# A first batch that loads keys and queries before values, softmaxes half of its heads without a subtraction pass and mixes heads in pairs, and a last row finished by columns

## The chip, the cores and the metric

The kernel runs on one core of a Trainium2 chip. The metric is the device time of one execution in microseconds (us). Before the change three runs took 468.88, 469.86 and 471.57 us; the median is 469.86 us. TensorE (PE in the profile) multiplies matrices and writes to PSUM; VectorE (DVE) and ScalarE (ACT) work on PSUM and SBUF; GpSimd (POOL) issues the input loads, SyncE (SP) the output stores and the transposing transfers.

## What is computed

Linear attention with projected keys and values, followed by two ReLU mixers, for 8 batches, 8 heads, 1024 rows and a head width of 64:

```python
k_proj = np.einsum('ks,bhsd->bhkd', E, k)      # 1024 rows of keys become 64
v_proj = np.einsum('ks,bhsd->bhkd', F, v)
scores = scale * np.matmul(q, k_proj.transpose(0, 1, 3, 2))
scores = scores - np.max(scores, axis=-1, keepdims=True)
attn = np.exp(scores)
attn = attn / (np.sum(attn, axis=-1, keepdims=True) + 1e-09)
x = heads_joined(np.matmul(attn, v_proj))      # 1024 x 512 per batch
h = np.maximum(x.T @ w_tok1, 0.0) @ w_tok2     # mixes the 1024 rows
u = x + h.T
out = u + np.maximum(u @ w_ch1, 0.0) @ w_ch2   # mixes the 512 columns
```

All inputs are float32 in memory; the loads turn them into bf16, and all products are in bf16 with float32 sums.

## The kernel before, in words

Each batch has two stages. `front(b)` runs from the loads of k, v and q to u and its transpose uT; `channel(b)` is the column mixer and the store. The 1024 rows lie as 128 partitions by NSI = 8, and pairs of these eight share a 128-wide tile (NT = 4).

**Front of the first batch.** Its loads come in chunks of two heads (`CHUNKS0`), in the order k, q, v for each chunk (L272). E and F are loaded by SP (L329), cast (L339), transposed (L347) and copied to `EFT_sb` (L351). `project_first` makes the key projection (L449, copied to `kbd` at L465) and the value projection (L457, copied to `vbd` at L470); each value product is made twice, for the upper and the lower 64 partitions of PSUM, with 64-column weights. `attend(h)` transposes q on PE (L484, copied at L494), makes the scores (L501), takes the row maximum (L510) and subtracts it (L511) on DVE, takes the exponential on ACT (L517), and transposes the result on PE (L536, copied to eT at L539). Heads then come in `GROUPS` of three, three and two: `sums_of` (L558) gives the row sums, which `invert` turns into 1/(sum + 1e-9) (L545, L546); `weigh` (L578) multiplies eT by the projected values, and a multiplication on DVE (L590) writes x. `tok1` (L610) mixes rows for the group's columns, `tok2_of` (L640) mixes them back and adds x by one more product with the identity (L644); its result is copied to u (L653), transposed (L665) and copied to uT (L672).

**Fronts of the other batches** take all eight heads, transpose exponentials and u by transposing transfers on SP's queue (L528, L701), from batch 2 on q too (L726), and add x on DVE (L691).

**Channel.** `up(sj, cc)` (L791) multiplies four rows of tiles by a 128-column slice of w_ch1; the ReLU writes gT (L247 on ACT, L249 on DVE). `down(si)` (L810) sums 12 products with w_ch2 into a full 512-column bank; DVE adds u (L820), SP stores 256 KB (L825).

**What sets the order.** Nothing runs in program order by itself. Each step is an `op` with the engines that may take it, an assumed duration, the ops it needs, and a priority; `Planner.plan` simulates the engines and the load queue with these assumed costs, picks the op that can start earliest (ties by priority), assigns buffers and PSUM banks, and writes out one fixed order for each engine. On the chip an engine follows this order whatever the true durations are. A front has priority level 2b, a channel 2b + 3; inside the first front a `rank` moves whole steps ahead or back (`RK`). All loads hang on one another in the order in which they are made (`load`, `behind`), and go through POOL's one queue: first batch, w_tok1, w_tok2, both halves of w_ch1 (L287), batch 1 in halves of four heads, and then loads held back by a gate (`later`), a one-element copy on POOL (L306) that waits for a late step: w_ch2 (L311) behind the first batch's uT, batch 2 behind the last eT of batch 1, and so on.

Of the kernel before, what the change touches and what calls it, by code (L numbers as in the profile page):

```python
# [10 lines left out]
BF16 = mybir.dt.bfloat16  # L11
# [3 lines left out]


# [43 lines left out]
class Planner:  # L60
# [19 lines left out]
    def plan(self, start):  # L80
# [7 lines left out]
        dma = 4.5  # L88
        ready = [o for o in self.ops if not o.waiting]
        order = []  # L90
        while ready:
# [28 lines left out]
            elif e == "PE":  # L120
                free[e] = t + w
                end = t + w + AFTER[e] + (SLACK if o.prio[0] > 0 else 0.0)
            elif e == "SP":
                free[e] = t + w
                dma = max(t + 1.0, dma) + o.dma
                end = dma + 1.0 + (DMA_SLACK if o.prio[0] % 2 == 0 else 0.0)
            else:
                free[e] = t + w - 0.08
                end = t + w + AFTER[e] - 0.08 + (SLACK if o.prio[0] > 0 else 0.0)
# [16 lines left out]
def kernel(  # L146
# [33 lines left out]
    RK = (-4, 3, 60)  # L180
# [27 lines left out]
    EFT_sb = sb.tile([P, NSI, 2 * KP], BF16, name="EFT_sb")  # L208
# [72 lines left out]
    CHUNKS0 = [(h, h + 2) for h in range(0, H, 2)]  # L281
    for c in CHUNKS0:
        for w in "kqv":
            load_in(0, w, *c, prio=(0, len(pl.ops)))

# [3 lines left out]
    ld_wt1 = load_w(wt1_sb, moe_w_tok1.rearrange("(p si) t -> p si t", p=P), S * DT * 4)  # L289
    ld_wt2 = load_w(wt2_sb, moe_w_tok2.rearrange("(tc p) s -> p tc s", p=P), S * DT * 4)  # L290
    ld_wc1 = []
    for c in range(0, DC, DC // 2):
        cs = slice(c, c + DC // 2)
        ld_wc1.append(load_w(
            wc1_sb[:, :, cs], moe_w_ch1.rearrange("(dc p) c -> p dc c", p=P)[:, :, cs], DM * DC * 2))
    CHUNKS1 = [(0, H // 2), (H // 2, H)]
    for c in CHUNKS1:
        for w in "kvq":
            load_in(1, w, *c, prio=(0, len(pl.ops)))

    ld_wc2 = []

    def later(b, whats, buf, of, dep):

        if b < B:
            gate = op({"POOL": 0.1}, lambda e: nc.gpsimd.tensor_copy(out=mark, in_=of()), [dep], [],  # L306
                      [buf], prio=(2 * b - 2, 0, len(pl.ops)))
            for w in whats:
                if w == "w":
                    ld_wc2.append(load(  # L310
                        lambda: nc.gpsimd.dma_start(  # L311
                            out=wc2_sb, in_=moe_w_ch2.rearrange("(cc p) d -> p cc d", p=P)),
                        (0, len(pl.ops)), DM * DC * 4, [gate]))
                else:
                    load_in(b, w, 0, H, (2 * b - 2, 0, len(pl.ops)), [gate])

# [5 lines left out]
    eft = []  # L322

    def staged(dt):
# [6 lines left out]
            (), [stage] if i == 0 else [], [stage], (-1, i), 0.3)  # L331
        for i, w in enumerate((E, F))
    ]
    for g in range(2):
# [9 lines left out]
        def ef_t(e, g=g, pb=pb):  # L344
# [7 lines left out]
            out=EFT_sb[:, sl, :], in_=b16(pb, 4, P)), [o], [], [pb], prio=(0, -9, g)))  # L352
# [7 lines left out]
    def front(b):  # L360
# [20 lines left out]
        def project(h0, h1):  # L381
# [54 lines left out]
            for h in range(h0, h1):  # L436
                kbd_at[h] = last

        def project_first(h0, h1):
# [14 lines left out]
            def vmm(e):  # L454
                for si in range(NSI):
                    for r in range(2):
                        nc.tensor.matmul(  # L457
                            f32(vb_, n * D)[r * KP : (r + 1) * KP], EFT_sb[:, si, KP : 2 * KP],
                            vin_.t[:, h0:h1, si, :], start=(si == 0), stop=(si == NSI - 1),
                        )  # L460
# [3 lines left out]
            for r in range(2):  # L464
                ok = op(either(n * KP, "f32"), lambda e, r=r: copier(e)(  # L465
                    out=bd.t[0][r * KP : (r + 1) * KP, a, :, r * KP : (r + 1) * KP],
                    in_=f32(kb_, n, KP)[r * KP : (r + 1) * KP]), [ok], [], [kb_, bd], pr())
            ov = op({"PE": 0.1 * NSI}, vmm, eft + [landed[b, "v", h0]], [vb_], [vin_, bd], pr())
            for r in range(2):
                ov = op(either(n * D, "f32"), lambda e, r=r: copier(e)(  # L470
                    out=bd.t[1][r * KP : (r + 1) * KP, h0:h1, r * SU : r * SU + D],
                    in_=f32(vb_, n, D)[r * KP : (r + 1) * KP]), [ov], [], [vb_, bd], pr())
            for h in range(h0, h1):
                kbd_at[h] = ok
                v_at[h] = [ov]

        def attend(h):
# [28 lines left out]
            os_ = op({"PE": 0.056 * NT}, scm, [oq, kbd_at[h]], [sc, mx, sh, ex], [qT, bd], pr())  # L506
# [15 lines left out]
            om = op({"DVE": 2 * dve(512) + 0.06}, smax, [os_], [], [sc, mx, sh], pr())  # L522

            oe = op({"ACT": act(512)}, expo, [om], [], [sh, ex], pr())
# [16 lines left out]

        sums_at, rdG = {}, {}
# [5 lines left out]
        def sums_of(g):  # L548
            heads = GROUPS[g]
# [19 lines left out]
        def weigh(g, t):  # L569
            heads = GROUPS[g]  # L570
            n = len(heads)
            pb = Buf(bankA)
            rd = rdG[g] if first else Buf(rd_pool)
# [6 lines left out]
            new = [pb] + ([] if first else [rd]) + ([xb] if (g, t) == (0, 0) else [])  # L580
# [3 lines left out]
            def norm(e):  # L584
                ou = f32(pb, n, 2 * SU).rearrange("p n (s d) -> p n s d", s=2)
                c = t * 2 * n if first else 0
                r = rd.t[:, c : c + 2 * n].rearrange("p (n s o) -> p n s o", s=2, o=1)
                if not first:
# [6 lines left out]
            x_at[g, t] = op({"DVE": (0 if first else 0.41) + dve(n * 128)}, norm,  # L595
# [7 lines left out]
        def tok1(i, heads):  # L603
# [11 lines left out]
            deps = [x_at[g, t] for g, hs in enumerate(GROUPS) for t in range(NT) if set(hs) & set(heads)]  # L615
# [13 lines left out]
        def tok2_of(heads):  # L629
# [3 lines left out]
            for s0 in range(0, NSI, per):  # L633
                pb = Buf(bankA)

                def mm(e, s0=s0, pb=pb):
                    up_ = f32(pb, per, n)
                    for s_ in range(per):
                        for i in range(TC):
                            nc.tensor.matmul(  # L640
                                up_[:, s_, :], wt2_sb[:, i, s0 + s_ :: NSI],
                                hb.t[:, i, a * D : z * D], start=(i == 0), stop=False,
                            )
                        nc.tensor.matmul(  # L644
# [230 lines left out]
```

## Time and profile before

| What | Value |
|---|---|
| median of three runs | 469.86 us |
| profiled execution: its own time, its span | 470.42 us, 468.6 us |
| PE busy, share of the span | 452.0 us, 96% |
| DVE, ACT, POOL busy | 265.7, 177.8, 35.5 us |
| up products L791, down products L810 | 768 each, 128x512 |
| HBM read, written | 59.24 MB, 16.78 MB |
| granted TensorE clock | 1.000 |

The span runs from the first instruction to the last; the profiled execution's own time is 1.8 us longer. A group line of the profile gives code line, engine, operation, tiles written and read, shape and count, and then the busy time, the mean duration of one in ns, and the idle time of the engine just before them with what ended it. A piece of the timeline gives its start and length in us. The busy time of PE is a union of modelled durations, each about 0.2 us with the pipeline's latency, so that close small gaps between products are covered by it; the number of products in a stretch says more. The mark "POOLq" or "SPq" is an instruction that issues a transfer.

### The profile page before, as it was taken

To read this page: it belongs to the slowest core of one execution; us is meant where nothing else is said; L and a number is where in the kernel's file an instruction comes from. 1 tells how busy PE (TensorE), PEld (TensorE's weight loads), DVE (VectorE), ACT (ScalarE), POOL (GpSimd) and SP (SyncE) were. 2 spreads that over 40 slices of the span, in tenths; PEclk is the share of its full clock that TensorE was granted. 3 is DMA by queue.
4 is the path that set the end of the run, shared out by engine and by line. 5 is a ranking of instruction groups with operands and counts; after the bars stand their busy time and mean duration, and the time that the engine had idled before them with its cause. 6 is when DMAs were issued, how large, how long until landed. Compare 5 with 4: busy or idle time off the path is not lost.

```text
span 468.6 us, 7476 instructions
## 1 busy us (share of the span) xinstructions
PE 452.0 (96%) x2908; PEld 236.3 (50%) x2908; DVE 265.7 (57%) x597; ACT 177.8 (38%) x324; POOL 35.5 (8%) x59
## 2 busy tenths in 40 slices
PE   2799999999999999999999999999999999999996
PEld 2686554444544455545544455545554455544442
DVE  3883884537645578537745499527844297521022
ACT  2866761127310671127510373116720375105600
POOL 7520010010000100010000100010000000000000
PEclk9999999999999999999999999999999999999999
DMA  8999949999899987979399996799488221451022
GB/s 157 207 209 207 191 69 194 230 158 227 99 210 185 179 125 129 202 153 203 50 197 149 188 165 98 168 182 224 87 151 189 90 57 34 65 160 46 1 90 91
DMA packets 122580, 68.14 MB, mean 145 GB/s; under 512 B 86704, under 2 KB 113840, under 8 KB 122544
## 3 DMA queue, kind: packets, MB, share of 16 engines
q0 software_dynamic: 28176, 29.36, 40.1%
q1 hardware_dynamic: 94368, 38.29, 38.4%
q8 instruction: 23, 0.38, 0.3%
q14 instruction: 13, 0.11, 0.1%
HBM read 59.24 MB, written 16.78 MB: 162 GB/s over the span
## 4 chain that ended last, share of the span: by engine, by line
PE 93%; DMA 2%; DVE 2%; POOL 1%; issue 1%; ACT 0%; POOLq 0%; DVEq 0%
PE bank L791 36%; PE bank L810 35%; PE bank L610 6%; PE bank L682 5%; PE bank L578 3%; PE bank L501 3%; PE bank L388 3%; DMA in<-in_v_dram 2%; POOL in L272 1%; DVE x L590 1%; PE bank L640 1%; PE bank L484 0%; PE bank L421 0%; PE bank L665 0%; DVE sh L511 0%
## 5 line engine op out<-in xcount | busy, mean ns | idle before, releaser
L791 PE MATMUL bank<-uT,wc_sb 128*128 128x512 bf16 x768 | 179.1, 379 | 0.0
L810 PE MATMUL bank<-wc_sb,gT 128*128 128x512 bf16 x768 | 173.9, 379 | 0.0
L247 ACT ACTIVATE gT<-bank 128x512 bf16<-128x512 f32 x166 | 98.7, 595 | 87.2 <-PE bank L791 87.2
L810 PEld LDWEIGHTS <-gT 128*128 128x128 bf16 x768 | 73.7, 98 | 84.5 <-issue 1.2
L791 PEld LDWEIGHTS <-wc_sb 128*128 128x128 bf16 x768 | 71.6, 98 | 74.2 <-issue 1.2
L820 DVE TENSOR_TENSOR o<-bank,u 128x512 f32<-128x512 f32 x64 | 43.9, 688 | 110.3 <-PE bank L810 110.3
L510 DVE TENSOR_REDUCE mx<-bank 128x8 f32<-128x512 f32 x64 | 43.6, 681 | 27.5 <-PE bank L501 27.4
L590 DVE TENSOR_TENSOR x<-bank,rd 128x384 bf16<-128x384 f32 (+1 forms) x96 | 48.5, 512 | 3.1
L691 DVE TENSOR_TENSOR u<-bank,x 128x512 bf16<-128x512 f32 x56 | 34.4, 680 | 23.7 <-PE bank L682 23.7
L511 DVE TENSOR_TENSOR sh<-bank,mx 128x512 f32<-128x512 f32 x64 | 44.3, 692 | 5.0 <-ACT ex L517 0.5
L517 ACT ACTIVATE ex<-sh 128x512 bf16<-128x512 f32 x64 | 40.1, 627 | 5.8 <-DVE sh L511 3.7
L402 ACT CAST kp<-bank 64x512 bf16<-64x512 f32 (+1 forms) x8 | 4.2, 525 | 90.9 <-PE bank L392 90.9
L247 ACT ACTIVATE hT<-bank 128x512 bf16<-128x512 f32 (+2 forms) x19 | 9.9, 523 | 64.9 <-PE bank L610 64.8
L610 PE MATMUL bank<-x,wt_sb 128*128 128x512 bf16 (+2 forms) x160 | 29.6, 336 | 0.0
L682 PE MATMUL bank<-hT,wt_sb 128*128 128x512 bf16 x112 | 25.3, 379 | 0.0
L249 DVE TENSOR_SCALAR gT<-bank 128x512 bf16<-128x512 f32 x26 | 17.8, 687 | 11.9 <-PE bank L791 11.4
L578 PEld LDWEIGHTS <-eT 128*128 128x128 bf16 x256 | 18.6, 97 | 11.2 <-DMA eT<-ex 0.2
L578 PE MATMUL bank<-vbd,eT 128*128 128x130 bf16 x256 | 23.1, 220 | 0.0
L501 PEld LDWEIGHTS <-qT 128*128 128x128 bf16 x256 | 17.8, 98 | 10.2 <-ACT qT L494 0.6
L501 PE MATMUL bank<-kbd,qT 128*128 128x128 bf16 x256 | 21.8, 219 | 0.5 <-ACT qT L494 0.5
L610 PEld LDWEIGHTS <-wt_sb 128*128 128x128 bf16 x160 | 14.6, 98 | 13.4
L682 PEld LDWEIGHTS <-wt_sb 128*128 128x128 bf16 x112 | 16.1, 144 | 8.4
(63 smaller groups left out, 214.1 us busy)
## 6 DMA issues: line engine op xcount, KB each, us to landing
out_dram<-o SPq DMA_DIRECT2D x64, 256.0 KB, 2.7
in<-in_k_dram POOLq DMA_DIRECT2D x6, 1024.0 KB, 11.0
in<-in_v_dram POOLq DMA_DIRECT2D x6, 1024.0 KB, 15.5
in<-in_q_dram POOLq DMA_DIRECT2D x6, 1024.0 KB, 9.7
wc_sb<-in_moe_w_ch_dram POOLq DMA_DIRECT2D x2, 768.0 KB, 17.2
wc_sb<-in_moe_w_ch_dram POOLq DMA_DIRECT2D x1, 1536.0 KB, 26.4
in<-in_k_dram POOLq DMA_DIRECT2D x4, 256.0 KB, 8.4
in<-in_q_dram POOLq DMA_DIRECT2D x4, 256.0 KB, 8.9
```

What stands on the lines that cost most here:

```text
L247: nc.scalar.activation(out=out, in_=in_, func=ACT.Relu)
L501: nc.tensor.matmul(f32(sc, NT, 2 * KP)[:, t, :], qT.t[:, h, t, :], bd.t[0][:, h // 2, h % 2, :], start=True, stop=True,)
L510: nc.vector.reduce_max(out=mx.t, in_=s_, axis=AX.X)
L511: nc.vector.tensor_tensor(out=sh.t, in0=s_, in1=mx.t[:, :, None].to_broadcast([P, NSI, KP]), op=ALU.subtract,)
L517: nc.scalar.activation(out=ex.t, in_=sh.t.rearrange("p (t s) k -> p t (s k)", s=2), func=ACT.Exp, scale=scale,)
L578: nc.tensor.matmul(ou[:, i], eTs[h].t[:, t, :], bd.t[1][:, h, :], start=True, stop=True)
L590: nc.vector.tensor_tensor(out=xb.t[:, t, heads[0] : heads[0] + n], in0=ou[:, :, :, 0:D], in1=r.to_broadcast([P, n, 2, D]), op=ALU.mult,)
L610: nc.tensor.matmul(f32(pb, n), wt1_sb[:, si, i * P : (i + 1) * P], xrow(si, a, z), start=(si == 0), stop=(si == NSI - 1),)
L682: nc.tensor.matmul(f32(pb, DM), wt2_sb[:, i, si::NSI], hb.t[:, i, :], start=(i == 0), stop=(i == TC - 1),)
L791: nc.tensor.matmul(f32(pb, 4, P), wc1_sb[:, dc, cc * P : (cc + 1) * P], uT.t[:, sj * 4 : (sj + 1) * 4, dc, :], start=(dc == 0), stop=(dc = ...
L810: nc.tensor.matmul(f32(pb, DM), g.t[:, cc, (si % 4) * P : (si % 4 + 1) * P], wc2_sb[:, cc, :], start=(cc == 0), stop=(cc == CC - 1),)
L820: nc.vector.tensor_tensor(out=ob.t, in0=f32(pb, DM), in1=u.t[:, si, :], op=ALU.add)
```

## The change

Parts, in the order of the code:

1. **Load order** (`LOADS`). First batch: q1, k0, q0, k1, k3, k2, v1, q3, v0, q2, then w_tok1, v2, v3, w_tok2, the first half of w_ch1, then batch 1 (k, v, q of the first four heads; v, k, q of the others), and only then the second half of w_ch1.
2. **Later loads** (`GATES`). w_ch2 comes in two halves, one behind the first batch's uT, one behind head 0's eT of batch 1; batch 2 comes behind head 4's eT of batch 1 instead of head 7's. The others keep their places.
3. **Value projection** of the first batch: one product with 128-column weights for two with 64 columns. `EFT_sb` holds F twice for it (two added copies).
4. **Exponentials** of heads 3, 4, 6 and 7 of the first batch (`DIRECT`): DVE takes the maximum and multiplies the 128x8 result by -scale; ACT then takes eight exponentials of 128x64 straight from PSUM with that result as bias. The subtraction is gone.
5. **Pairs** (`GROUPS0`): four groups of two heads for three of three, three and two; row sums for each (`SUMMED`).
6. **Adding x** in groups 0 and 3 (`ADDED`): by DVE on the way from PSUM to u, in two pieces of 256 a bank, for the identity product and a copy.
7. **The last row** of the last batch (`down_by_columns`): 256, 128 and 128 columns, each with its own 12 products, addition and store.
8. The ranks, some assumed costs of the planner, and the dependences of the two halves of `kbd` and `vbd` (both halves now follow the product, before one followed the other). `front(b + 1)` is described to the planner before `channel(b)`.

```diff
+LOADS = ("q1", "k0", "q0", "k1", "k3", "k2", "v1", "q3", "v0", "q2", "wt1", "v2", "v3", "wt2",
+         "wc1a", "K0", "V0", "Q0", "V1", "K1", "Q1", "wc1b")
+GROUPS0 = ((0, 1), (2, 3), (4, 5), (6, 7))
+DIRECT = (3, 4, 6, 7)
+ADDED = (0, 3)
+SUMMED = (0, 1, 2, 3)
+RK = (-30, -3, 63)
+GATES = {(0, "u"): ("w0",), (1, 0): ("w1",), (1, 4): ("v2", "k2", "q2"), (1, "u"): ("k3", "v3"),
...
-    RK = (-4, 3, 60)
...
             def vmm(e):
                 for si in range(NSI):
-                    for r in range(2):
-                        nc.tensor.matmul(
-                            f32(vb_, n * D)[r * KP : (r + 1) * KP], EFT_sb[:, si, KP : 2 * KP],
-                            vin_.t[:, h0:h1, si, :], start=(si == 0), stop=(si == NSI - 1),
-                        )
+                    nc.tensor.matmul(
+                        f32(vb_, n * D), EFT_sb[:, si, KP : 3 * KP],
+                        vin_.t[:, h0:h1, si, :], start=(si == 0), stop=(si == NSI - 1),
+                    )
...
+            def rmax(e):
+                nc.vector.reduce_max(out=mx.t, in_=f32(sc, NSI, KP), axis=AX.X)
+                nc.vector.tensor_scalar(
+                    out=mx.t, in0=mx.t, scalar1=-scale, scalar2=None, op0=ALU.mult)
+
+            def expo_direct(e):
+                s_ = f32(sc, NSI, KP)
+                for si in range(NSI):
+                    nc.scalar.activation(
+                        out=ex.t[:, si // 2, (si % 2) * KP : (si % 2 + 1) * KP], in_=s_[:, si, :],
+                        func=ACT.Exp, bias=mx.t[:, si : si + 1], scale=scale,
+                    )
...
+            if first and h in DIRECT:
+                om = op({"DVE": dve(512) + 0.2}, rmax, [os_], [], [sc, mx], pr())
+                oe = op({"ACT": NSI * 0.15 + 0.08}, expo_direct, [om], [], [sc, mx, sh, ex], pr())
...
+                def add(e, s0=s0, pb=pb):
+                    for s_ in range(0, per, 2):
+                        w = min(2, per - s_)
+                        nc.vector.tensor_tensor(
...
+        def down_by_columns(si, widths):
...
+            for w in widths:
...
+                    for cc in range(CC):
+                        nc.tensor.matmul(
+                            f32(pb, cs.stop - cs.start), g.t[:, cc, (si % 4) * P : (si % 4 + 1) * P],
+                            wc2_sb[:, cc, cs], start=(cc == 0), stop=(cc == CC - 1),
+                        )
...
+                op({"SP": 0.1}, lambda e, cs=cs: nc.sync.dma_start(
+                    out=out.rearrange("b (p si) d -> b p si d", p=P)[b, :, si, cs], in_=ob.t[:, cs]),
...
+            if (b, si) == (B - 1, NSI - 1):
+                down_by_columns(si, (DM // 2, DM // 4, DM // 4))
```

## The prediction

> **What bounds the kernel now.** I read the busy shares and the slices first. Columns of the first lines: busy us, share, instructions; below, tenths of busy time in 40 slices of 11.7 us.
>
> ```profile
> PE 452.0 (96%) x2908; PEld 236.3 (50%) x2908; DVE 265.7 (57%) x597; ACT 177.8 (38%) x324; POOL 35.5 (8%) x59
> PE   2799999999999999999999999999999999999996
> DVE  3883884537645578537745499527844297521022
> ACT  2866761127310671127510373116720375105600
> ```
>
> PE is full from the fourth slice to the last but one; the first three and the last are what is open. The busy time by stretches then says where (columns: stretch, length, busy us and count for PE, weight loads, DVE, ACT, POOL, clock, DMA share, GB/s):
>
> ```profile
> 5.00:10.00 5.00, 1.53 (x13) 1.27 (x14) 1.32 (x3) 2.39 (x2) 4.04 (x6) 1.00 1.15 173
> 10.00:15.00 5.00, 4.55 (x116) 4.03 (x115) 2.22 (x5) 3.38 (x10) 2.65 (x4) 1.00 1.24 205
> 15.00:20.00 5.00, 3.40 (x89) 2.76 (x84) 4.58 (x9) 4.39 (x10) 2.25 (x4) 1.00 1.24 205
> 20.00:25.00 5.00, 4.45 (x107) 3.94 (x104) 4.72 (x12) 4.18 (x10) 2.26 (x4) 1.00 1.12 213
> 25.00:30.00 5.00, 4.71 (x67) 4.40 (x68) 4.83 (x11) 3.36 (x9) 1.48 (x2) 1.00 1.15 210
> 30.00:35.00 5.00, 4.80 (x72) 4.59 (x69) 3.37 (x10) 3.06 (x8) 1.19 (x2) 1.00 1.18 207
> 35.00:40.00 5.00, 4.65 (x71) 4.36 (x70) 1.50 (x4) 3.87 (x8) 0.00 (x0) 1.00 1.25 210
> 60.00:440.00 380.00, 379.32 (x2124) 188.93 (x2123) 221.44 (x506) 135.16 (x236) 17.69 (x29) 1.00 0.78 143
> ```
>
> From 60 to 440 us PE idles 0.7 us in all; nothing there can be shortened but by taking products away. From 15 to 30 us DVE is 94% busy (14.1 of 15 us), ACT 80%, and the loads run at a steady 205 GB/s. So the first front is bound first by arriving loads, then by DVE. The timeline shows where it ends: the last transposes of u, and the first product of the channel stage at 39.92 us.
>
> ```profile
> 39.69 0.40 PE L665 MATMUL bank<-ident,u 128*128 128x128 bf16 x4 [0.35 <-ACT u L653]
> 39.92 0.38 PE L791 MATMUL bank<-uT,wc_sb 128*128 128x512 bf16 x1
> ```
>
> From then on PE always has something, so every us by which the first front ends earlier is a us of the total, as long as the work behind it has its data. At the end, the chain of waits and the timeline show the other open piece:
>
> ```profile
> 443.88 20.73 PE bank L810 x96
> 464.63 0.69 DVE o L820
> ```
>
> The last addition ends at 465.32, its store lands about 2.0 us after its issue (transfers by stretches), and the span ends at 468.6.
>
> **The loads, part 1.** Issue time plus time to landing, asked load by load, gives for the first batch 7.3 (k0), 8.9, 10.2, 11.5, 12.7, 14.0, 15.3, 16.65, 19.05, 20.3, 21.5 and 22.9 us (v3), then w_tok1 25.5, w_tok2 27.85, the halves of w_ch1 31.55 and 35.3, batch 1's six pieces 37.8, 40.4, 42.9, 45.4, 48.0 and 50.5, w_ch2 59.5. POOL issues as many transfers of the same sizes in the same queue, so I put the new order on these slots: the last query chunk (q2) lands at 20.3 instead of q3 at 21.5, w_tok1 at 22.9, v2 and v3 at 24.2 and 25.5 (2.6 us later than v3 before), w_tok2 again at 27.85, w_ch1's first half at 31.55, batch 1 from 34.1 to 46.9 (each 3.7 us earlier), w_ch1's second half at 50.5 instead of 35.3. Scores of heads 2, 3 can start 1.2 us earlier; heads 0, 1, whose q0 moves from 8.9 to 10.2, lose little, since their keys wait for EFT (copied until 10.15) and their scores started at 12.88.
>
> **PE work, parts 3, 5, 6.** The value projection saves nothing: 16 paired half-width products took 0.64 us, 8 full-width ones (L484, the x8 piece) 0.61. The identity products of two groups go: 3 products per row of tiles took 0.247 us at 192 columns, so tok2 cost 16 x 0.082 + 8 x 0.056 = 1.77 us there and costs 16 x 0.056 = 0.90 in a pair: with the columns regrouped, 16 products of 128 are saved, 0.9 us. Tok1 handles the same columns in 64 products instead of 48. None of this binds before 32 us; it is a part of the earlier end below, not added to it.
>
> **DVE and ACT until the last x.** The stretch 10 to 33.8 us holds 19.71 us of DVE and 17.65 of ACT. DVE changes: four subtractions at 0.69 go, four 128x8 multiplications come (nearest row: 128x24, 0.17; I take 0.15), -2.2; 16 multiplications of 0.42 for 8 of 0.55 and 4 of 0.42, +0.6; a fourth inversion, +0.3; two copies of F (nearest row 0.29 for 64x256 bf16), +0.5; additions of group 0, 2 banks x 2 x 0.42, +1.7. Sum 20.6. ACT: eight exponentials of 128x64 are not in the trace. From above: the 64x128 cast, 0.258 each without overlap, 2.06 a head. From below: the ACT rows at 128 and 512 columns (0.277, 0.595) make 0.17 + 0.00083 a column, 0.22 at 64, and two copies in a row (1.07 for two of 0.585) overlap by 0.10, so 0.12 each, 0.96 a head. I take 0.18, in the middle, 1.45 a head: 4 x (1.45 - 0.63) = +3.3; the four copies of group 0's u at 0.477 go to DVE, -1.9. Sum 19.0. So DVE stays the longer one, 0.9 us longer than before, but it starts fuller: in 10 to 15 us it idled 2.8 us for want of scores, and with four heads' q and k there by 12.7 instead of 14 to 16 I expect half of that; with the other 1.3 us of idle time kept, 10 + 20.6 + 1.4 + 1.3 = 33.3, less 0.5 for copies that ACT (19.0 of 23) can take: last x at 32.8 instead of 33.8.
>
> The Trainium skill (ScalarE: Activation LUTs, What ACT_TABLE_LOAD costs) says that an activation whose bias is a per-partition operand takes about 280 ns + 0.833 ns a column, and that neighbours overlap by about 93 ns. That is an estimate of 0.24 us each and 1.9 a head; the 512-column rows here (0.595 to 0.63) lie near the 0.61 that it gives without such an operand and below the 0.71 with one, so no row here shows the surcharge. By the rule ACT would hold 20.8 us, and the third rival below would be near.
>
> **From the last x to the channel stage.** Before, 33.8 to 39.9, 6.1 us, because PE was still busy with the second group's tok1 and tok2 (32.0 to 35.9). With pairs, that work is done two heads at a time and earlier; w_tok2's landing at 27.85 plus 64 + 16 products at 0.056 (4.5 us) ends at 32.4, before the last x is through. What remains is serial: tok1 16 x 0.056 + 0.17 = 1.1, ReLU 0.28, tok2 0.9, addition or copy 0.58 to 0.84, transposes 0.4, copy 0.5: 3.9 us. The channel stage starts at **36.7** instead of 39.9: -3.2. Bounds: 35.2 (exponentials at the low end, last x 1.5 earlier) and 39.3 (at the high end, 4 x 0.6 = 2.4 us more on ACT).
>
> **What the moved half of w_ch1 costs.** Until 50.5 us PE has 12 ups of 4 x 0.216, 10.4 us, and of batch 1 two projections of 0.9, queries and scores of 0.9 for each half: some 14 us for 13.8. I take 0.2 us of idling. If nothing of batch 1 came in time, PE would have done 10.4 us by 50.5, where it did 10.6 before: the move can eat the gain, not turn it into a loss. The split of w_ch2 lands at or after 54.5 and about 59.5, as before; 10.4 us of ups cover 50.5 to 59.5. Batch 2's loads (part 2), released at 67.75 before, come some 8 us earlier.
>
> **The last row, part 7.** PE needs 24 products of 128 more than half as many of 256 do: 12 x (0.109 + 0.056 + 0.056) = 2.65 for 2.59 us, +0.06. The last addition falls from 0.69 to 0.29 (0.42 at 256 columns, 0.69 at 512, carried on), -0.4. The last store moves 64 KB instead of 256: packets of the last 256 KB ran some 0.8 us, so between nothing and 0.6 is saved; I take 0.4. Together -0.75.
>
> The Trainium skill (DMA: Bandwidth & Descriptors, two cost components) gives 2.0 us fixed plus bytes at 436 GB/s; by it the store saves an estimate of 0.45. The trace's 2.0 us for a whole 256 KB store is below its 2.6, so the fixed part is smaller here.
>
> **Sum.** -3.2 + 0.2 - 0.75 = -3.75 us on the profiled execution's 470.42 (span 468.6 and 1.8 around it): 466.67. That execution lay 0.56 above the median of the runs, 469.86, so the forecast is **466.1 us**, own range 464.0 to 467.5.
>
> **Rivals.**
> 1. *The front ends little earlier.* DVE has more to do, not less (20.6 for 19.7), and v3 comes 2.6 us later; if the order holds DVE no fuller than before, the last x stays at 33.8 or slips to 34.5, and only the shorter tail of PE work remains, an end near 38.8. For it: 94% of DVE. Against it: its idle 2.8 us at 10 to 15. 470.42 - 1.1 - 0.75 - 0.56 = 468.0 us. Chance 0.24.
> 2. *The forecast*, 0.62, with ends down to 35.2 (464.4) in it.
> 3. *ScalarE becomes the bound.* Each direct head waits for 2.06 us of ACT where the plan assumed 1.28; ACT cannot hand exponentials on, and qT and eT copies are queued behind them, as PE's transposes of later heads are behind the ones that wait. 4 x 0.78 = 3.1 us late on ACT, and the same again when PE's and DVE's fixed orders wait for the late eT: the channel starts at 36.7 + 6.2 = 42.9, 470.42 + 3.0 - 0.75 - 0.56 = 472.1 us. It turns to a loss when the front ends after 40.65, at 1.94 a head, 0.24 an exponential. For it: ACT already at 80%. Against it: 4 us of ACT are idle before 33.8. Chance 0.14. The skill's rule named above gives this break-even price almost exactly.
>
> **Numbers.** A measurement of this kernel can tell about 0.5% (2.35 us) from no change: faster is below 467.5, slower above 472.2. Rival 1 straddles the first bound, rival 3 the second with its worse half: faster 0.62, same 0.25, slower 0.13. Range 463.8 to 470.8: it takes in the forecast and rival 1 and leaves out most of rival 3.
>
> **What would show it.** The first L791 product near 36.7 us; DVE above 90% from 12 us; an exponential of 64 columns at 0.15 to 0.2 us apart; last x near 33; w_ch1's second half landing near 50 with PE idle under 1 us from 37 to 60; a last addition of 0.3 us and a span that ends 3.2 us after the last product instead of 4.0. Wrong would be a channel start at or after 39, or PE gaps beyond 60 us.

## The result, and the profile after

The changed kernel takes **476.31 us** in the median of six runs (474.33 to 478.84), where 466.1 was forecast: 1.0137 times the time before, with a 95% interval of 1.0101 to 1.0173. It is slower by 6.5 us, and the range given (463.8 to 470.8) doesn't hold it. The profiled execution took 476.23 us, its span 474.4: 5.8 us more than before. A run more than 1.5% longer than the shortest of its kernel is left out of the medians and ratios below: one of e2 (476.32 us), four of e4 (481.07 to 482.50) and one of the kernel before (535.93).

The top of the page of after, its busy line and the slices of PE and ACT:

```profile
PE 452.3 (95%) x2895; PEld 238.3 (50%) x2924; DVE 267.6 (56%) x618; ACT 179.6 (38%) x345; POOL 36.3 (8%) x61
PE   2899998996999999999999999999999999999996
ACT  2886841044510373116621184114730185105600
```

PE's row, all nines from the fourth slice to the last but one before, now has an 8 in the seventh slice and a 6 in the tenth (71 to 83 and 107 to 119 us). That is far behind the first front, in a part of the kernel that the prediction took to be full. What PE waited for after 50 us (line waited at, releaser, total, times, longest):

```profile
PE bank L524 <- DMA qT<-in: 4.2, 1, 4.2
PE bank L619 <- DMA eT<-ex: 1.1, 1, 1.1
```

Before, only a wait of 0.7 us stood in that stretch. The chain of waits of after shows both at their places (start, length, what):

```profile
63.80 8.97 DMA eT<-ex
...
94.74 18.76 DMA qT<-in
...
113.55 0.61 PE bank L524 x4
```

The second is the larger one. A transposing transfer of batch 2's q, half of it (four heads), took 18.8 us to land; the first half took 4.6, and before the change the two took 5.6 and 7.8. What is queued around it is seen in the timeline of SP and POOL (start, us, engine, line, operation):

```profile
91.18 1.76 SPq L783 DMA_TRANSPOSE qT<-in  x1
93.03 1.62 SPq L907 DMA_DIRECT2D out_dram<-o  x2
94.74 9.60 SPq L783 DMA_TRANSPOSE qT<-in  x1
```

```profile
93.19 0.18 POOL L327 COPY mark<-uT 1x1 bf16<-1x1 bf16 x1 [27.08 <-DMA uT<-u]
93.64 0.88 POOL L286 DMA_DIRECT2D in<-in_k_dram  x1 [0.28 <-issue]
```

Batch 3's k and v are held back until batch 1's uT is complete. That now comes at 93.19, between the two halves of q. So two loads of 1 MB each (as written) are issued 1.1 and 0.2 us ahead of the second half (k at 93.64, v at 94.51), and even the instruction that issues the half stays blocked for 9.6 us. Before the change, SP and POOL had it the other way round (the second line is the second half, which is also part of the first):

```profile
93.41 5.43 SPq L726 DMA_TRANSPOSE qT<-in  x2
96.98 1.87 SPq L726 DMA_TRANSPOSE qT<-in  x1
97.27 0.18 POOL L306 COPY mark<-uT 1x1 bf16<-1x1 bf16 x1 [26.39 <-DMA uT<-u]
97.81 0.88 POOL L272 DMA_DIRECT2D in<-in_k_dram  x1 [0.36 <-issue]
```

Both halves were issued first, but the second only 0.8 us ahead of k's load. PE pays twice. Stretches of after (columns as in the table of before, the clock third from the end):

```profile
112.00:114.00 2.00, 0.45 (x5) 0.45 (x6) 0.00 (x0) 0.00 (x0) 0.00 (x0) 0.83 0.86 241
114.00:116.00 2.00, 2.00 (x10) 0.90 (x8) 1.38 (x2) 0.10 (x1) 0.00 (x0) 0.50 0.98 202
116.00:118.00 2.00, 2.00 (x11) 0.95 (x10) 1.38 (x2) 1.54 (x4) 0.00 (x0) 0.82 0.00 0
118.00:120.00 2.00, 2.00 (x14) 1.03 (x13) 1.33 (x2) 2.00 (x5) 0.00 (x0) 1.00 0.41 84
```

After the gap the granted clock is 0.50, and 1.00 again from 118 on; from 114 to 118 that costs 2 x 0.50 + 2 x 0.18 = 1.4 us, and 1.6 with the 0.45 us from the end of the gap to 114. So 4.2 + 1.6 + 1.1 = 6.9 us are lost here, more than the 5.8 by which the span grew. By this count the rest of the change gained 1.1 us in this execution.

The front itself, by the stretches of after:

```profile
10.00:15.00 5.00, 4.68 (x102) 4.25 (x101) 2.87 (x7) 2.23 (x6) 2.57 (x5) 1.00 1.24 205
15.00:30.00 15.00, 12.58 (x236) 10.60 (x230) 12.92 (x37) 14.79 (x54) 5.76 (x8) 1.00 1.17 209
```

From 15 to 30 us ACT, the fourth pair, is busy 14.8 of 15 us, where DVE led before with 14.1; DVE is down to 12.9. The timeline of after has the last x, and the first product of the channel stage:

```profile
32.96 1.41 DVE L631 TENSOR_TENSOR x<-bank,rd 128x256 bf16<-128x256 f32 x4
40.70 1.03 PE L848 MATMUL bank<-uT,wc_sb 128*128 128x512 bf16 x4
```

The last x ends at 34.4 (before 33.8), and the channel starts at 40.7 (before 39.9).

### The profile page after: what moved, and what is told of

It reads as the page before. It is cut to its first block, busy times and chain, and to the rows that moved or that the text cites. A ratio compares the mean times of both kernels' runs of the same rounds, so it can differ in the third digit from the quotient of the medians.

```text
span 474.4 us, 7540 instructions
## 1 busy us (share of the span) xinstructions
PE 452.3 (95%) x2895; PEld 238.3 (50%) x2924; DVE 267.6 (56%) x618; ACT 179.6 (38%) x345; POOL 36.3 (8%) x61
## 4 chain that ended last, share of the span: by engine, by line
PE 87%; DMA 7%; ACT 3%; issue 1%; DVE 1%; SPq 0%; ACTq 0%
PE bank L848 33%; PE bank L891 32%; PE bank L651 5%; PE bank L739 5%; DMA qT<-in 4%; PE bank L524 3%; PE bank L619 3%; PE bank L412 2%; DMA eT<-ex 2%; DMA gT<-in_F_dram 1%; ACT ex L553 1%; PE bank L681 1%; PE bank L507 1%; ACT ex L540 1%; PE bank L722 0%
## 5 line engine op out<-in xcount | busy, mean ns | idle before, releaser
L848 PE MATMUL bank<-uT,wc_sb 128*128 128x512 bf16 x768 | 181.6, 381 | 0.1
L891 PE MATMUL bank<-wc_sb,gT 128*128 128x512 bf16 x729 | 168.4, 379 | 1.4 <-issue 0.2
L261 ACT ACTIVATE gT<-bank 128x512 bf16<-128x512 f32 x170 | 101.0, 595 | 129.8 <-PE bank L848 128.8
L891 PEld LDWEIGHTS <-gT 128*128 128x128 bf16 x756 | 72.8, 98 | 85.9 <-issue 2.5
L533 DVE TENSOR_REDUCE mx<-bank 128x8 f32<-128x512 f32 x60 | 41.0, 684 | 20.2 <-PE bank L524 20.1
L534 DVE TENSOR_TENSOR sh<-bank,mx 128x512 f32<-128x512 f32 x60 | 41.5, 692 | 4.9
L540 ACT ACTIVATE ex<-sh 128x512 bf16<-128x512 f32 x60 | 37.6, 627 | 4.7 <-DVE sh L534 3.5
L651 PE MATMUL bank<-x,wt_sb 128*128 128x512 bf16 (+1 forms) x176 | 29.9, 321 | 0.0
L524 PE MATMUL bank<-kbd,qT 128*128 128x128 bf16 x256 | 22.9, 224 | 4.7 <-DMA qT<-in 4.2
L261 ACT ACTIVATE hT<-bank 128x512 bf16<-128x512 f32 (+1 forms) x18 | 9.7, 536 | 41.0 <-PE bank L651 41.0
L651 PEld LDWEIGHTS <-wt_sb 128*128 128x128 bf16 x176 | 14.8, 98 | 13.2
L263 DVE TENSOR_SCALAR gT<-bank 128x512 bf16<-128x512 f32 x22 | 15.1, 688 | 8.8 <-PE bank L848 8.3
## 6 DMA issues: line engine op xcount, KB each, us to landing
in<-in_v_dram POOLq DMA_DIRECT2D x4, 256.0 KB, 10.6
```

The source lines that it names most:

```text
L261: nc.scalar.activation(out=out, in_=in_, func=ACT.Relu)
L524: nc.tensor.matmul(f32(sc, NT, 2 * KP)[:, t, :], qT.t[:, h, t, :], bd.t[0][:, h // 2, h % 2, :], start=True, stop=True,)
L533: nc.vector.reduce_max(out=mx.t, in_=s_, axis=AX.X)
L534: nc.vector.tensor_tensor(out=sh.t, in0=s_, in1=mx.t[:, :, None].to_broadcast([P, NSI, KP]), op=ALU.subtract,)
L540: nc.scalar.activation(out=ex.t, in_=sh.t.rearrange("p (t s) k -> p t (s k)", s=2), func=ACT.Exp, scale=scale,)
L651: nc.tensor.matmul(f32(pb, n), wt1_sb[:, si, i * P : (i + 1) * P], xrow(si, a, z), start=(si == 0), stop=(si == NSI - 1),)
```

## The experiments

The theory, after reading the two traces: the earlier release of batch 3's k and v puts them ahead of q's transposing transfer, and this collision is the loss. The rivals were that the first front itself comes out later (the direct exponentials, the load order), and that the two stores which now stand between the halves of q delay the second one. Each ratio below is to the kernel before, run on the same chip beside it, whose median was 469.97 to 470.53 us.

**e1: the loads of batch 3 wait for q's transposes.** One gate moved, nothing else.

```diff
-GATES = {(0, "u"): ("w0",), (1, 0): ("w1",), (1, 4): ("v2", "k2", "q2"), (1, "u"): ("k3", "v3"),
+GATES = {(0, "u"): ("w0",), (1, 0): ("w1",), (1, 4): ("v2", "k2", "q2"), (2, "q"): ("k3", "v3"),
...
+            later((b, "q"), qTb, lambda: qTb.t[0:1, 4, 0, 0:1], o)
```

> The changed kernel with one edit: the loads of keys and values of batch 3 wait for the second half of batch 2's q transposes, no longer for batch 1's uT. Theory 'collision' (the 18.8 us landing of that half, issued just after those loads, starves PE by 4.2 us and half the clock for some 4 us costs 1.7 more): that half lands in 5 to 7 us, no PE wait over 1 us at 108 to 114 us, granted clock 1.000, 470.4 us. Rival 'spread' (the earlier loads of batch 2, the late eT and a slower first front cost a little everywhere): 474 us or more, stall or no stall. Rival 'front' (the new first batch loses what is lost): 476 us.

Measured: 468.44 us, ratio 0.9975 [0.9954, 0.9995]; the span of the profiled execution 466.6 us, at a clock of 1.000. The timeline of e1, SP and then POOL:

```profile
90.89 3.03 SPq L783 DMA_TRANSPOSE qT<-in  x1
94.02 1.01 SPq L908 DMA_DIRECT2D out_dram<-o  x2
95.12 3.46 SPq L783 DMA_TRANSPOSE qT<-in  x1
```

```profile
101.19 0.88 POOL L286 DMA_DIRECT2D in<-in_k_dram  x1 [0.28 <-issue]
```

The same two stores stand between the halves, which land 5.0 and 5.5 us after issue, and no wait of PE beyond 50 us is left in the list. So the stores alone are not the cause, and with the collision the loss is gone: 7.8 us of span between the two executions. Not all of the 7.8 is the gate's. The wait of 1.1 us for eT is missing too, and the channel starts at 40.1 instead of 40.7, both at places ahead of the release that was moved.

**e2: both halves of q in one step,** so that no store and no load comes between them; the gates as in the change.

```diff
-            for h0 in range(0, H, 4):
-                o = op({"SP": 3.5}, lambda e, h0=h0: nc.sync.dma_start_transpose(
...
+            def both(e):
+                for h0 in range(0, H, 4):
+                    nc.sync.dma_start_transpose(
...
+            o = op({"SP": 7.0}, both, [landed[b, "q", 0]], [qTb], [qin, qTb], pr(), dma=8 * S * D * 2 / TURN)
```

> The changed kernel with one edit: both halves of a batch's q transposes are one step of the plan, so that no store stands between them on SP. Theory 'collision': the second half is issued before the loads of batch 3 take the queues, lands in 5 to 8 us, 470.4 us. If the loads hit it all the same, although it is issued first: landing over 12 us and 474 to 476 us. Rival 'front': 476 us.

Measured: 469.70 us, ratio 0.9997 [0.9981, 1.0013]; span 467.6. SP issues the two from 91.48 on, 5.38 us for both, the second at 94.64, and POOL k's load at 95.53; the halves land in 5.3 and 9.0 us. The stall of PE is gone with q ahead of the loads, whichever way this is reached. The stores matter only as far as they put the second half behind the loads. e2 is 1.3 us above e1, with intervals that overlap; of the 1.0 us between the two spans 0.9 lie ahead of anything the edit touches (the channel starts at 41.0, in e1 at 40.1).

**e3: the new gates alone,** in a kernel that otherwise has the load order, groups, exponentials, ranks and last row of before (it keeps the full-width value projection and the planner's new costs).

```diff
-GROUPS0 = ((0, 1), (2, 3), (4, 5), (6, 7))
-DIRECT = (3, 4, 6, 7)
-ADDED = (0, 3)
+LOADS = ("k0", "q0", "v0", "k1", "q1", "v1", "k2", "q2", "v2", "k3", "q3", "v3", "wt1", "wt2",
+         "wc1a", "wc1b", "K0", "V0", "Q0", "K1", "V1", "Q1")
+GROUPS0 = ((0, 1, 2), (3, 4, 5), (6, 7))
+DIRECT = ()
+ADDED = ()
...
-RK = (-30, -3, 63)
+RK = (-4, 3, 60)
...
-            if (b, si) == (B - 1, NSI - 1):
+            if False:
```

> Only the changed gates of the later loads (and the full-width value projection); the first batch's load order, groups, exponentials, addition of x and the last row are those of before. Theory 'collision': the plan has the same two stores between the halves of q, so the stall is there too if the timing of batch 1 is alike: 474 to 477 us, second half landing over 12 us. Rival 'front': no loss without the new first front, 470 us.

Measured: 485.58 us, ratio 1.0339 [1.0304, 1.0374]. PE waits 7.5 us for qT, whose second half was issued at 100.73, 1.0 us behind batch 3's k, and landed 19.3 us later; and 4.0 us for eT. Without the new first batch the gates cost over twice as much as with it. So the first batch isn't what made the kernel slower.

**e4: the first batch alone,** with the old places of w_ch2 and batch 2.

```diff
-GATES = {(0, "u"): ("w0",), (1, 0): ("w1",), (1, 4): ("v2", "k2", "q2"), (1, "u"): ("k3", "v3"),
+GATES = {(0, "u"): ("w0", "w1"), (1, 7): ("k2", "v2", "q2"), (1, "u"): ("k3", "v3"),
```

> The changed kernel with the gates of before for w_ch2 and batch 2 (both halves of w_ch2 behind the first batch's uT, batch 2 as k, v, q behind head 7's eT); first batch and last row as changed. Theory 'collision': q of batch 2 lands some 4 us later than in the changed kernel, its halves are issued before the loads of batch 3 or land late with one store between; without the stall 470 to 471 us, what is left is what first batch and last row are worth, within 1 us of nothing. Rival 'front': 475 to 477 us.

Measured: 471.19 us, ratio 1.0032 [1.0015, 1.0050]; the profiled execution, with a span of 471.3, is the longest of the six. In it PE waits 1.5 us for qT (halves landing in 5.4 and 11.5 us) and 0.9 for v. The second half was issued at 101.35 and batch 3's k at 101.41: a dead heat.

**e7: the kernel before, with batch 3's k and v released earlier.** The test from the other side: nothing of the change, only this release.

```diff
-        later(b + 2, "w" if first else "kv", uTb, lambda: uTb.t[0:1, NSI - 1, 0, 0:1], uT_at[b][NSI - 1][-1])
+        sg = 1 if b == 1 else NSI - 1
+        later(b + 2, "w" if first else "kv", uTb, lambda: uTb.t[0:1, sg, 0, 0:1], uT_at[b][sg][-1])
```

> The kernel before with one edit: the loads of batch 3's keys and values wait for the first two of eight tiles of batch 1's uT instead of the last, so they are issued some 5 us earlier, ahead of the q transposes of batch 2. Theory 'collision': one or both q halves land in over 12 us instead of 5.6 to 6.7, PE waits 2 to 7 us for them near 103 to 112 us and then runs at half clock for a few us: 473 to 479 us. Rival (the stall belongs to the changed plan, not to loads ahead of a transposing transfer): 470 us, halves under 8 us.

Measured: 480.4 us, ratio 1.0216 [1.0195, 1.0238]. The timeline of e7:

```profile
91.83 0.88 POOL L272 DMA_DIRECT2D in<-in_k_dram  x1 [0.36 <-issue]
```

```profile
94.29 16.81 SPq L726 DMA_TRANSPOSE qT<-in  x2
```

its chain of waits, with the first half alone:

```profile
94.29 17.25 DMA qT<-in
```

and PE's waits and its stretches:

```profile
PE bank L501 <- DMA qT<-in: 8.8, 1, 8.8
```

```profile
108.00:112.00 4.00, 0.41 (x5) 0.41 (x6) 0.00 (x0) 0.00 (x0) 0.00 (x0) 0.50 1.25 226
112.00:116.00 4.00, 4.00 (x18) 2.05 (x17) 3.45 (x6) 1.11 (x2) 0.00 (x0) 0.51 0.89 308
```

Here no store stands between the halves of q. The first is issued 2.5 us behind k and lands in 17.3 us; its instruction stays blocked for 12.6 us, so the second is issued only at 107.0, and lands in 6.2. 8.8 us of waiting and 4 x 0.49 = 2.0 us at half clock make 10.8, and the span grew by 10.6 (479.2 for 468.6). Loads ahead of the transposes are enough by themselves.

**e5 and e8: no direct exponentials.** e5 is e1 with `DIRECT = ()`; e8 is e5 with the last row as in e6 below.

> The kernel of e1 (batch 3's keys and values behind q's second half) with one more edit: no head of the first batch takes its exponentials straight from PSUM (the subtraction is back for heads 3, 4, 6, 7). Theory 'ScalarE bound' (eight exponentials take 1.75 us where one took 0.63, ACT is 98% busy from 15 to 30 us): ACT falls by 4.5 us there, DVE rises by 2.1, the last x comes up to 1 us earlier, 467.4 to 468.4 us against e1's 468.4. Rival 'DVE bound': DVE is again 94% busy and the first front ends 1 us later, 469 to 470 us. A change of the plan's order elsewhere (q's transposes go ahead of uT's) may cost or give some tenths.

> e1 with both edits of e5 and e6. If both theories hold and add up: 466.8 to 467.8 us, 0.5% under the kernel before. Rival 'DVE bound': 468.5 to 469.5 us.

Measured: 473.88 us, 1.0072 [1.0051, 1.0092], and 472.79 us, 1.0057 [1.0038, 1.0076]. The plan came out in another order, with q's transposes ahead of uT's, and PE waits for k, eT and uT (2.2, 1.8 and 1.5 us in e5). They don't price the exponentials; a kernel with its order kept was needed.

**e9: subtraction, in the order and with the buffers of e6.** Every engine keeps its sequence; only what the two steps do is put back, for heads 3, 4, 6 and 7.

```diff
-                om = op({"DVE": dve(512) + 0.2}, rmax, [os_], [], [sc, mx], pr())
-                oe = op({"ACT": NSI * 0.15 + 0.08}, expo_direct, [om], [], [sc, mx, sh, ex], pr())
+                om = op({"DVE": dve(512) + 0.2}, smax, [os_], [], [sc, mx], pr())
+                oe = op({"ACT": NSI * 0.15 + 0.08}, expo, [om], [], [sc, mx, sh, ex], pr())
```

> The kernel of e6 with every engine's order and all buffers kept, but heads 3, 4, 6 and 7 of the first batch do the subtraction on DVE (0.69 us) and one exponential on ACT (0.63) where e6 has the 128x8 multiplication (0.17) and eight exponentials (1.75). This takes the plan's reshuffling of e5 out. Theory 'ScalarE bound': ACT falls from 98% to about 80% between 15 and 30 us, the first front's last transposes of u come up to 1 us earlier, 467.4 to 468.4 us against e6's 468.4. Rival 'DVE bound': DVE above 93% there, the front ends 0.5 to 1.5 us later, 469 to 470 us.

Measured: a median of 473.48 us over 12 runs, 1.0035 [0.9996, 1.0074], in two groups: 468.34 to 470.68 (3 runs) and 472.17 to 475.29 (9). The profiled execution is of the first, span 466.5, against 466.3 of e6. From 15 to 30 us, e6 and then e9:

```profile
15.00:30.00 15.00, 12.57 (x218) 10.59 (x217) 13.11 (x38) 14.78 (x55) 5.79 (x8) 1.00 1.17 209
```

```profile
15.00:30.00 15.00, 11.49 (x211) 10.13 (x209) 14.39 (x36) 10.50 (x26) 5.90 (x8) 1.00 1.17 209
```

The direct form takes 1.3 us from DVE (third pair) and puts 4.3 on ACT (fourth). The last x ends at 33.9 with it and 34.1 without, and the spans differ by as much, 0.2 us: that is all that the subtraction's removal gives to the front in these two executions. The longer group is another matter (e13).

**e13: e9's kernel once more,** for the trace of one of its longer runs.

> The kernel of e9 once more, for a profile of the slower kind of its executions. Theory 'second collision': a PE wait of 2 to 5 us for eT<-ex at 70 to 78 us, landing of head 7's eT 8 us or more, the granted clock under 1.0 in the stretch behind it, no other wait over 1.5 us after 40 us. Rival: the wait is elsewhere. If the execution is of the faster kind (468 to 470.7 us), the look tells nothing new.

Measured: 474.58 us, span 472.7. Its waits and two of its stretches:

```profile
PE bank L619 <- DMA eT<-ex: 2.8, 1, 2.8
```

```profile
76.00:78.00 2.00, 2.00 (x11) 1.12 (x10) 1.43 (x6) 0.00 (x0) 0.00 (x0) 0.50 1.23 205
78.00:80.00 2.00, 2.00 (x8) 0.73 (x6) 0.85 (x2) 0.00 (x0) 0.00 (x0) 0.67 1.24 205
```

This is the smaller wait of the change's own trace, larger: batch 2's loads, released behind head 4 of batch 1 (POOL issues them from 64.31 on), slow the last eT transposes of the same batch. Head 7's eT lands in 10.7 us; before the change the last one took 2.4.

The first batch has a part in it, which the rival of the next experiment also names. From 15 to 30 us e13 has

```profile
15.00:30.00 15.00, 12.50 (x224) 11.39 (x218) 13.65 (x32) 10.35 (x25) 5.95 (x8) 0.89 1.17 209
```

with a granted clock of 0.89 where e9's shorter execution and e6 had 1.00, and its channel starts at 42.0 instead of 40.5. These 1.5 us, the wait of 2.8 and 2 x 0.50 + 2 x 0.33 = 1.7 at the lower clock make 6.0 of the 6.2 us between the two spans. The later front also brings the collision about: head 7's eT is issued at 65.12 instead of 63.56, while the mark behind head 4 moves only from 63.54 to 63.80. So the loads, 0.5 us behind this eT in e9, are 0.8 us ahead of it here. How much of the 1.5 us is the clock's isn't shown (PE also waited 0.6 us longer for E and F at the start), and the other eight long runs have no trace.

**e12: e9 with batch 2 released behind head 7,** as before the change.

```diff
-GATES = {(0, "u"): ("w0",), (1, 0): ("w1",), (1, 4): ("v2", "k2", "q2"), (2, "q"): ("k3", "v3"),
+GATES = {(0, "u"): ("w0",), (1, 0): ("w1",), (1, 7): ("v2", "k2", "q2"), (2, "q"): ("k3", "v3"),
```

> The kernel of e9 with one more edit: batch 2's loads wait for head 7's eT of batch 1 instead of head 4's. e9's executions fell into two kinds, 468.3 to 470.7 us at a clock of 1.000 and 472 to 475 at 0.992 to 0.995. Theory 'second collision' (batch 2's loads, issued before the last eT transposes of batch 1, stretch them to 9 us or more, as in the changed kernel and in e11, and whether PE then waits long enough to lose its clock hangs on a few tenths): with the later release all executions lie within 2 us of each other, clock 0.998 or more, 468.5 to 471 us, with PE waiting up to 1.5 us for batch 2's values. Rival (the two kinds come from the first batch): two kinds again.

Measured: 470.69 us, 0.9998 [0.9978, 1.0018]; 11 runs from 468.76 to 471.90, batch 2 released at 68.27 in the trace, no wait for eT, and no run above 472. With the release behind head 7 the times of e9 above 472 are gone, so these had the second collision in them. But the expectation (all within 2 us, clock 0.998 or more) wasn't met, and the rival is right in part: four runs took 468.76 to 469.71 us at a clock of 0.999, and six 470.34 to 471.90 at 0.996 (the eleventh 471.08 at 1.000). The profiled one is of the longer kind:

```profile
15.00:30.00 15.00, 12.21 (x215) 11.07 (x214) 13.33 (x32) 10.26 (x24) 5.69 (x8) 0.89 1.17 209
```

Its clock falls in the first front as in e13, and its channel starts at 42.7, 2.2 us later than in e9's; the span is 2.9 longer. In e6 and e10, which have the direct exponentials, all 23 runs had a clock of 0.999 or 1.000. So the direct exponentials give 0.2 us where the clock stays up, but in e9 and e12, without them, it often didn't: the medians of e9 and e6 are 473.48 and 468.44 us.

**e11: the load order of before,** all else as in e6.

> The kernel of e6 with the first batch's loads, weights and batch 1 in the order of before. If the new load order is what shortens the first front: its last transposes of u come 1 to 3 us later than in e6 (40 us), PE idles more before 30 us, 469.5 to 471.5 us. Rival (the order of the loads matters little, since DVE and ACT bound the stage): 468 to 469 us.

Measured: 475.60 us, 1.0092 [1.0064, 1.0121]; span 471.0 in the profiled execution, the shortest of its 12 runs. PE waits 3.7 us for eT: head 7's eT is issued after batch 2's loads (64.36) and lands 9.3 us later. That wait is 3.7 of the 4.7 us by which the span exceeds e6's. Against the expectation, the first front isn't later: its last transposes of u end at 40.1 (e6: 40.4), and PE is busy 17.7 of 20 us from 10 to 30 (17.6). The new load order is needed, in this kernel, mostly so that batch 1's transposes are through before batch 2's loads.

**e10: e6 with the old places of w_ch2 and batch 2.**

> The kernel of e6 (batch 3's keys and values behind q's second half, row pieces last) with w_ch2 and batch 2 released as before (both halves of w_ch2 behind the first batch's uT, batch 2 as k, v, q behind head 7's eT). Theory 'collision': e4's 473.0 us falls to 469 to 470.5, its q half lands in under 8 us, what is left over e6 is the later landing of batch 2 (PE waited 0.9 us for its values in e4). Rival (e4 was slow for another reason): 472 to 473 us.

Measured: 470.14 us, 0.9975 [0.9949, 1.0001]; q's halves land in 5.4 and 4.5 us, PE waits 1.1 us for v. By the two medians (470.14 and 470.53 us) the ratio is 0.999. With batch 3 behind q's transposes, and the pieces of the last row last, the first batch no longer loses anything (e4: 1.0032). Whether the earlier release of batch 2 gains beyond that isn't settled: the intervals of e6 and e10 overlap.

**e6: e1, and the pieces of the last row wait for the row ahead of it.**

```diff
-                o = op({"PE": CC * (0.003 + w / 2400)}, mm, list(ld_wc2.values()) + [g_at[sj, cc] for cc in range(CC)],
+                o = op({"PE": CC * (0.003 + w / 2400)}, mm, [row_done, *ld_wc2.values()] + [g_at[sj, cc] for cc in range(CC)],
...
-                down_by_columns(si, (DM // 2, DM // 4, DM // 4))
+                down_by_columns(si, (DM // 2, DM // 4, DM // 4), row_done)
```

> The kernel of e1 with one more edit: the column pieces of the last row start after all products of the row before it. Theory 'interleaved tail' (row 6's last four products and its 256 KB store stand between the pieces, so that the end is still a whole row's): last piece's addition 0.3 us after the last product, no other store within 2 us of the end, the end of the span 3.2 to 3.4 us after the last product instead of 3.9, 467.8 us against e1's 468.4. Rival 'fixed cost' (a store takes as long whatever its size): only the shorter addition counts, 0.3 to 0.4 us, 468.1.

Measured: **468.44 us** (467.80 to 469.57, 11 runs), 0.9961 [0.9949, 0.9973]: the best version, ahead of both kernels. Why the row needed this is in the timeline of the changed kernel, which had its last products so:

```profile
469.03 0.81 PE L891 MATMUL bank<-wc_sb,gT 128*128 128x512 bf16 x3
469.68 0.83 PE L870 MATMUL bank<-wc_sb,gT 128*128 128x128 bf16 x12
469.88 0.69 DVE L902 TENSOR_TENSOR o<-bank,u 128x512 f32<-128x512 f32 x1 [0.57 <-PE bank L891]
```

The full-width row ahead (L891) ends between the pieces (L870), so its addition of 0.69 us stands just before the last small one, and its 256 KB store just before the last small store. From PE's end to the span's end it takes 3.9 us (before 4.0). In e6 the row is through first:

```profile
462.91 0.29 DVE L878 TENSOR_TENSOR o<-bank,u 128x128 f32<-128x128 f32 x1 [0.38 <-PE bank L871]
```

and 3.4 us pass to the end. Its last stores, of 128 and 64 KB, land in 1.8 and 1.6 us, where the last one of 256 KB took 2.0 before, so the rival 'fixed cost' doesn't hold. The 0.3 us by which the span is shorter than e1's can't be told apart in the medians, which are equal.

## Why the prediction was wrong, point by point

**The step that failed** is the one on the later loads: "Batch 2's loads (part 2), released at 67.75 before, come some 8 us earlier", costed at nothing. They came 4.8 us earlier, and the sum missed two things. The chain of releases behind them moved too: batch 3's k and v came at 93.2 instead of 97.3, which put them ahead of half of q's transposes. And a load that comes early isn't free: it lengthens each transposing transfer behind it, from 5 to 19 us for q and from 2.4 to 9 for an eT. Terms of the sum that should have been there: 4.2 us of stall for qT, 1.6 at half clock, 1.1 for eT. e1 shows the first two by taking them away, e7 by making them in the old kernel, e12 and e13 show the third. The prediction did name PE gaps beyond 60 us as what would make it wrong. It never looked for what might cause one: the profile of before had q's second half issued at 96.98 and the loads at 97.81, 0.8 us apart, much less than the shifts that the prediction itself forecast (3.2 us for the front, 8 for batch 2's loads).

**The front's gain** was also too large. e1 has the front without the collision: its last product ends at 462.7 where 464.6 stood before, so 1.9 us gained for 3.0 forecast (-3.2 and +0.2). With 0.9 of it for the identity products by the forecast's own count, about 1 us is left for all the rest. The terms, from the trace of after:
- DVE did 20.1 us of work from 10 us to the last x (20.6 forecast). From 10 to 15 us it had 2.87 of 5 us, where 3.6 were hoped for and 2.22 stood before; in e1 and e6 it had 3.3 and 3.2. But from 15 to 30 us it idled 2.1 us (2.0 in e1) where it had idled 0.9; 1.3 of them (1.2 in e1) it waited for ACT's half of `vbd`. The last x came at 34.4, in e1 at 33.8 and in e6 at 33.9, not 32.8.
- A direct head took 1.78 us of ACT, not 1.45, with the group of the 32 exponentials as witness:

```profile
L553 ACT ACTIVATE ex<-bank,mx 128x64 bf16<-128x64 f32 x32 | 7.1, 355 | 0.0
```

  7.1 / 4 is 1.78 a head. The bounds 0.12 to 0.258 for one beside others hold it (0.22), near the upper one. The Trainium skill (ScalarE: Activation LUTs, What ACT_TABLE_LOAD costs) gives 0.33 for a single one and 0.24 beside others: the trace has a median of 0.34 and (1.78 - 0.34) / 7 = 0.21. The rule was a better guide than the middle of the rows, and its surcharge for a per-partition bias is seen here.
- The channel start at 40.7 says less than the prediction made it say: the planner put batch 1's projection ahead of it (39.24, before at 40.88), and PE is 10.0 of 10 us busy from 30 to 40 in e1 (9.45 before). What counts is PE's end, not this product's start.

**The tail** was to give 0.75 us and gave 0.1, because the sum took the pieces to be the last work, and the plan mixed them with the row ahead. With them last (e6) it gives 0.6, with the 0.4 for the last store as forecast. The size was nearly right, its condition wasn't met.

**What held.** The loads landed as the slots said: q2 at 19.3 (20.3 forecast), w_tok1 21.3 (22.9), w_ch1's second half 49.3 (50.5). PE doesn't idle from 37 to 60 us, so moving half of w_ch1 cost nothing. The value projection saved nothing that shows.

**The rivals.** Rival 1, a front that ends little earlier, was nearest in kind: 468.0, and e1 and e6 measured 468.4 once the collision was out of the way. Rival 3 had the sign, and 472.1, for another reason: ACT did become the busiest engine of the front (14.8 of 15 us), but e9, with the load of ACT taken away, ends no earlier in its shortest run, and later in e13. The loss that came, a release moved onto a transposing transfer, was no rival at all.

**Open:** why the clock falls in the first front of e9's kernel in some executions and not in others; and why four of the six runs of the changed kernel had a mean clock of 0.991 where the profiled one had 0.996. No trace here settles either.

## What to carry to other kernels

A release that moves earlier is a transfer that goes ahead of others: list what is queued between its old place and its new one, and within a few us of the new one, down the whole chain of gates, and see whether one of these is a transfer that PE waits for. Tie bulk loads to the landing of the small transposing transfers that are needed sooner, not to an event that merely came later in the old timing. And when a last piece of work is made small, check that the plan still puts it last.

## What the runs showed of the hardware

A transposing transfer of 512 KB (half of batch 2's q) landed in 4.4 to 6.5 us with the next loads issued 2.5 us behind it or later. With two loads of 1 MB closer to it the time hung on when the first of them was issued: 0.8 us behind it 7.8 us (before), 0.9 behind 9.0 (e2), 0.1 behind 11.5 (e4), and 1.0 to 2.5 us ahead of it 17.3 to 19.3 (e3, the change, e7). Its issuing instruction was then blocked on SP for 9.6 to 12.6 us. The second half in e7, issued 15 us behind the loads, landed in 6.2 again. The last transfer of an eT, 128 KB, took 2.4 us with the loads 0.5 us behind it (e9), 5.4 and 5.5 with them 0.1 and 0.45 behind (e6, e1), and 9.0 to 10.7 with them 0.3 to 2.9 ahead (the change, e13, e3, e11).

A gap of PE is paid again: after 4.2 us (the change), 8.8 (e7) and 2.8 (e13) the clock was 0.50 in the next stretch of 2 to 4 us, and 1.00 by 3.5 to 4.5 us after the gap; a wait of 1.1 us in the trace of after cost no clock. Read in stretches of 0.5 us, it stayed at half for 3.4 us (the change, e13, and e3 after its 4.0 us), 6.8 (e3 around its 7.5 us) and 10.2 (e7, partly within the gap): one, two and three times the same length. The Trainium skill (TensorE: Matmul & The Clock Gate, What's actually happening) has a free-running window of about 3.4 us, after which an idle PE drops to half its clock and a busy one gets it back; the lengths of the slow parts agree. The gap of 2.8 us is shorter than the window that it gives, one of 3.7 us in e11 left the clock at 1.00 from 70 to 80 us, and in the first front of e13 it was at half for 3.4 us from 24.7 on with no single wait of PE above 1.2 us from 10 us on. So the length of one gap alone doesn't decide here.
